# A fused SSM and linear-attention kernel: three quarters of x transposed by DMA on its way in

## Chip, cores and metric

One core of one Trainium2 chip runs the whole computation in one launch. The metric is the device time of the launch in microseconds. The profile's engines are PE (TensorE), PEld (its weight loads), DVE (VectorE), ACT (ScalarE), POOL (GpSimd) and SP (SyncE, which here only issues transfers).

## What is computed

For an input x of 2048 tokens by 512 features in bf16, two branches are mixed by a gate per token.

```python
g = sigmoid((x * gate_w).sum(-1, keepdims=True))
# a: diagonal complex state-space model, 512 states
Bu = einsum("bld,pd->blp", x + 0j, B_bar)
h_t = Lam_bar * h_{t-1} + Bu_t                  # over 2048 tokens
a = 2.0 * einsum("blp,dp->bld", hseq, Cmat).real + x * Dskip
# b: linear attention, 32 heads of 16
q, k, v = split(x @ wqkv)
phi(u) = concat(softmax(u @ w_phi), softmax(-u @ w_phi))
b = (phi(q) @ (phi(k).T @ v)) / (phi(q) @ phi(k).sum(tokens) + 1e-6) @ wo
out = g * a + (1 - g) * b
```

## The kernel before

**Layout.** Tokens are numbered as (a, c, f): a block a of 4, a row c of 128 in it, and a residue f of 4, so token = (a*128 + c)*4 + f. Nearly every product needs x with features on the partitions. That is the tile `xT`, 128 partitions by 4 feature blocks by 2048 token columns; the 512 columns of one residue f stand together, and `tcols(f, a)` names 128 of them. The recurrence over tokens is folded by four: each residue class has its own local products, and a scan runs over the 512 groups.

**Loading x.** Five plain transfers on the SP queue (lines 312, 315, 317) bring x as it stands into `xn`: block 0 in two halves, then blocks 1 to 3, each partition taking four consecutive tokens (4 KB) of a block. Between them stands half of `Wv`, the V part of the projection; its other half is issued on the ACT queue (line 314). `x_block(a)` then transposes each of the 16 tiles of 128 tokens on TensorE, four 128x128 transposes into one PSUM bank (line 431), and a copy by ACT or DVE (lines 373 and 375) puts the bank into `xT`. After the first two tiles of block 0, one matmul on a blank tile `warm` (line 443) is put into PE's list. Six more stand before everything (line 418).

**Other loads.** Behind x, the SP queue holds the DMA transposes of the two B matrices into `BT` (line 321), the small `Wc`, the DMA transposes of the K and Q parts of the projection into `WT` (lines 323 and 324), `Wo` in four parts, and later the DMA transposes of the two C matrices (line 602). Five short parameter vectors go by the ACT queue (line 319), three more by POOL (line 334).

**Work on xT.** `v_unit(ti)` makes V for 128 tokens with four 512-column matmuls (line 457), where f = ti mod 4 and a = ti div 4. The gate needs sixteen one-column matmuls for each residue (line 904). `g_unit(j)` multiplies `BT` by all 512 columns of one residue, for each of the four residues in turn (line 685), and chains them by a diagonal product (line 690). `k_unit` makes the k features (line 797) and their products with V (line 828), `q_unit` the q features (line 888), and `mix` the outputs (lines 997, 1013, 1017, 1029). `fold` prepares the projection weights with w_phi (line 665) from `WT` and a block-diagonal matrix that DVE builds from `Wc`.

**What sets the order.** Every piece is a task with the engines that may run it, its costs, what it waits for, and its buffers. Transfers issued at the start stand for the plan as times, for instance `d_x = [pl.at(t) for t in (3.9, 5.6, 7.0, 8.6, 10.2)]`. The plan does not search: a written list `ORDER` names every task in turn (entry div 2) and its engine (entry mod 2, the first or second of those allowed), and the instructions are put out in that order. Each engine runs its own list in order and waits at the first instruction whose data is missing. The times in the plan choose buffers, but make nothing wait. Buffers named ET are four large tiles: x in natural order holds two of them at first, the tables' scratch and `WT` the other two; the C matrices take one when it is free, and q features use all four later.

Of the kernel before, what the change touches and what calls it, by code (L numbers as in the profile page):

```python
# [18 lines left out]
P = 128  # L19
# [103 lines left out]
def kernel(  # L123
# [48 lines left out]
NDUM = 1  # L172
ORDER = (
    8, 10, 14, 13, 26, 174, 22, 176, 18, 166, 170, 25, 21, 190, 173, 162, 17, 158, 169, 202, 192, 178, 206, 165,
    0, 194, 222, 204, 197, 226, 28, 224, 160, 209, 30, 230, 32, 198, 233, 250, 96, 210, 218, 234, 34, 201, 228,
    36, 40, 38, 214, 252, 180, 42, 242, 134, 212, 236, 44, 238, 46, 216, 4, 186, 136, 2, 48, 90, 59, 240, 254,
    244, 220, 812, 182, 62, 810, 140, 75, 188, 83, 61, 138, 678, 814, 142, 55, 184, 98, 69, 680, 430, 156, 434,
    144, 432, 816, 258, 146, 66, 56, 64, 436, 262, 438, 81, 342, 265, 818, 256, 334, 70, 260, 337, 346, 148, 348,
    338, 554, 150, 341, 444, 446, 344, 152, 52, 440, 154, 6, 450, 443, 356, 358, 360, 350, 382, 352, 354, 87, 388,
    50, 449, 362, 364, 85, 384, 820, 392, 528, 556, 522, 366, 390, 272, 386, 368, 394, 370, 490, 396, 372, 530,  # L180
    456, 398, 524, 458, 374, 532, 274, 400, 452, 496, 526, 376, 534, 78, 536, 460, 404, 822, 470, 538, 276, 406,
    414, 378, 92, 380, 540, 472, 462, 417, 408, 426, 454, 494, 544, 492, 266, 73, 475, 498, 500, 464, 284, 286,
    546, 410, 542, 502, 476, 298, 466, 412, 77, 504, 548, 620, 428, 100, 506, 508, 102, 288, 104, 88, 562, 268,
    468, 624, 614, 652, 512, 514, 622, 278, 618, 300, 106, 270, 516, 518, 616, 478, 290, 110, 626, 108, 280, 520,
    480, 282, 302, 628, 114, 656, 558, 630, 292, 418, 654, 112, 564, 550, 294, 246, 402, 482, 422, 304, 248, 566,
    560, 646, 116, 568, 738, 650, 648, 574, 484, 632, 118, 552, 486, 570, 576, 636, 424, 572, 580, 658, 594, 586,
    740, 296, 122, 742, 582, 660, 420, 638, 744, 584, 578, 306, 120, 746, 710, 94, 126, 686, 488, 596, 588, 598,
    124, 698, 640, 308, 310, 748, 688, 634, 690, 770, 130, 662, 750, 590, 510, 682, 700, 642, 128, 702, 684, 644,
    776, 664, 712, 774, 778, 838, 692, 668, 592, 752, 312, 772, 754, 314, 780, 782, 600, 714, 832, 694, 756, 670,
    704, 844, 672, 834, 760, 696, 602, 330, 842, 846, 784, 318, 706, 840, 132, 604, 666, 762, 850, 332, 836, 716,  # L190
    708, 718, 786, 720, 826, 322, 606, 788, 852, 722, 874, 854, 792, 848, 868, 320, 326, 794, 862, 674, 608, 724,
    764, 324, 796, 828, 872, 830, 328, 676, 766, 726, 768, 798, 800, 864, 878, 856, 876, 610, 866, 860, 728, 804,
    808, 870, 802, 892, 880, 894, 896, 806, 730, 758, 884, 904, 902, 900, 732, 858, 898, 906, 886, 1268, 908, 316,
    1000, 890, 882, 1270, 998, 910, 1036, 914, 996, 916, 1274, 1002, 734, 1272, 888, 918, 912, 1262, 920, 922,
    1028, 1004, 1054, 924, 1006, 930, 1074, 1062, 1030, 1022, 1008, 1010, 1056, 1128, 1130, 1076, 1080, 1024,
    1048, 1132, 1032, 612, 1264, 1050, 1256, 1126, 1058, 1026, 1266, 1078, 1082, 1100, 1102, 1034, 1012, 1052,
    1114, 932, 736, 1040, 1060, 1106, 1014, 1084, 1104, 1088, 1108, 1016, 1110, 1018, 1112, 1134, 1020, 1260,
    1038, 1086, 942, 936, 1116, 1136, 926, 1138, 934, 1066, 1276, 1064, 954, 1278, 1142, 944, 1092, 1118, 1204,
    1206, 1042, 1210, 1230, 1258, 938, 1232, 1068, 1236, 1208, 1212, 1234, 1044, 1214, 1090, 1152, 928, 1144,
    1146, 1158, 966, 1238, 1094, 1178, 1070, 1120, 1216, 940, 1154, 1218, 1122, 1280, 1148, 1096, 1222, 1240,  # L200
    1073, 1184, 1180, 1242, 1156, 946, 1186, 1284, 1166, 1282, 1160, 1244, 968, 1188, 1286, 1192, 948, 1288, 1246,
    1150, 1290, 1162, 1384, 1292, 1098, 1182, 1168, 1248, 1296, 1364, 1164, 1386, 970, 1190, 1358, 1125, 1170,
    1366, 1194, 1298, 1250, 1390, 956, 1300, 1360, 1220, 950, 958, 1392, 1302, 1224, 1368, 1196, 1312, 1046, 1306,
    1388, 1362, 1394, 1314, 1172, 1370, 1308, 952, 1338, 960, 1396, 1226, 1174, 1198, 1252, 1332, 1310, 1376,
    1200, 1372, 962, 1346, 1398, 1316, 1334, 964, 1400, 1318, 1340, 972, 1304, 1402, 1202, 1416, 1374, 1255, 978,
    1418, 1336, 1320, 1342, 1436, 980, 1438, 1344, 1378, 1404, 1324, 974, 1420, 1229, 1410, 976, 1442, 1380, 1348,
    982, 990, 1412, 1322, 1326, 1444, 1440, 1406, 1462, 1350, 1414, 1177, 984, 1383, 992, 1468, 1494, 1422, 986,
    1446, 1450, 1464, 1448, 988, 1470, 1428, 1352, 1328, 1496, 1354, 1488, 1476, 994, 1330, 1472, 1466, 1490,
    1424, 1454, 1474, 1140, 1498, 1409, 1492, 1500, 1480, 1356, 1426, 1478, 1452, 1430, 1433, 1456, 1482, 1435,
    1502, 1485, 1504, 1506, 790, 1294, 1458, 1514, 824, 1508, 1460, 1520, 1487, 1522, 1516, 1510, 1518, 1513, 1524)  # L210
# [18 lines left out]
def _fast_path(ctx, tc, A_x, A_Lambda_re, A_Lambda_im, A_B_re, A_B_im, A_C_re, A_C_im, A_log_dt, A_Dskip,  # L229
# [5 lines left out]
    x4 = A_x[0].rearrange("(a c f) d -> a c f d", f=F, c=P)  # L235
# [64 lines left out]
    xn2 = [wk.tile([P, 2, F, D], BF16, tag=f"ET{k}", name="xn", bufs=1) for k in range(2)]  # L300
    xn = [xn2[a // 2][:, a % 2] for a in range(4)]
# [10 lines left out]
    nc.sync.dma_start(out=xn[0][:, 0:2], in_=x4[0][:, 0:2])  # L312
    for k, q in ((0, nc.scalar), (2, nc.sync)):
        q.dma_start(out=Wv[:, k:k + 2, :], in_=B_wqkv[k * P:(k + 2) * P, 2 * D:3 * D].rearrange("(k p) n -> p k n", p=P))
    nc.sync.dma_start(out=xn[0][:, 2:4], in_=x4[0][:, 2:4])
    for a in range(1, 4):
        nc.sync.dma_start(out=xn[a], in_=x4[a])
# [26 lines left out]
    pl = _Plan({"DVE": 2.4e3, "ACT": 5.0e3, "PE": 1.1e3, "SP": 32.0e3})  # L344
# [10 lines left out]
    early = [pl.held("ET", k) for k in range(4)]  # L355
# [4 lines left out]
    def bfv(b):  # L360
        return b.t[:].bitcast(BF16)[:, 0:512]
# [17 lines left out]
    d_x = [pl.at(t) for t in (3.9, 5.6, 7.0, 8.6, 10.2)]  # L379
    d_wv, d_b, d_wk, d_wq, d_wo, d_ct = (pl.at(t) for t in (5.3, 19.5, 25.5, 30.5, 33.0, 0.0))  # L380
    d_wv0 = pl.at(4.4)
    d_vec, d_wc = pl.at(10.5), pl.at(21.0)
# [38 lines left out]
    xt = {}  # L421
    dums = []

    def x_block(a):
        pl.unit("x_block")
        for f in range(F):
            b = pl.buf(*A1)

            def tr(e, b=b, f=f):
                for kt in range(KT):  # L430
                    nc.tensor.transpose(bfv(b)[:, kt * P:(kt + 1) * P], xn[a][:, f, kt * P:(kt + 1) * P], ident[:])
            t = pl.add({"PE": 460.0} if a == 0 and f < 2 else _pe(4, 128), tr, deps=[d_x[a + (a > 0 or f > 1)]], follow=[t_warm], bufs=[b, early[a // 2]])
            if a == 0 and f < 2:
                dums.append(t)
            xt[a, f] = evac_task(xT[:, :, tcols(f, a)], b, lambda b: bfv(b).rearrange("p (k c) -> p k c", k=KT), [t],
                                 ("ACT", "DVE"), bf=True, rank=9)

        if a == 0:
            bd = pl.buf(*A1)

            def dum(e):
                for _ in range(NDUM):
                    MM(out=bd.t[:], lhsT=warm[:, 0:P], rhs=warm[:], start=True, stop=True)
            t_dum.append(pl.add({"PE": NDUM * 430.0}, dum, follow=dums, bufs=[bd]))

    vt = {}
    t_dum = []

    def v_unit(ti):
        pl.unit("v_unit")  # L450
        f, a = ti % F, ti // F
        b = pl.buf(*A1)

        def mm(k0, k1):
            def fn(e):
                for kt in range(k0, k1):
                    MM(out=f32v(b), lhsT=xT[:, kt, tcols(f, a)], rhs=Wv[:, kt, :], start=(kt == 0), stop=(kt == KT - 1))  # L457
            return fn
        if ti < 2:
            t = pl.add({"PE": 860.0 if ti == 0 else 434.0}, mm(0, 2), deps=[xt[a, f], d_wv0], follow=t_dum, bufs=[b])  # L460
            t = pl.add({"PE": 434.0}, mm(2, 4), deps=[d_wv], follow=[t], bufs=[b])
        else:
            t = pl.add(_pe(4, 512), mm(0, 4), deps=[xt[a, f], d_wv], bufs=[b])
        vt[ti] = evac_task(vx[:, ti, :, 0:Dh], b, lambda b: f32v(b).rearrange("p (h e) -> p h e", e=Dh), [t], ("ACT",), rank=8.5)

    x_block(0)
# [366 lines left out]
    x_block(1)  # L833
    for ti in range(0, 4):
        v_unit(ti)
    x_block(2)
# [858 lines left out]
```

## Time and profile before

| what | value |
|---|---|
| median of 13 runs | 154.75 us (153.97 to 155.31) |
| profiled execution's own time | 155.0 us |
| its span in the profile | 153.0 us |
| PE busy | 145.5 us (95%) |
| DVE busy | 134.3 us (88%) |
| ACT busy | 110.2 us (72%) |
| x transposes on PE, L431 | 64, first at 4.0 us, last at 18.0 us |
| first product with BT, L685 | 21.06 us |

The profile counts from the start of its span. The execution's own time is 2.0 us longer than the span, which lies around it. Busy time of PE overlaps a little with waiting, since the ends of pipelined matmuls are modelled. A busy share alone does not say what a change is worth; for that one has to see which wait ends last in the stage that is changed.

### The profile page before, as it was taken

To read this page: it belongs to the slowest core of one execution; us is meant where nothing else is said; L and a number is where in the kernel's file an instruction comes from. 1 tells how busy PE (TensorE), PEld (TensorE's weight loads), DVE (VectorE), ACT (ScalarE), POOL (GpSimd) and SP (SyncE) were. 2 spreads that over 40 slices of the span, in tenths; PEclk is the share of its full clock that TensorE was granted. 3 is DMA by queue.
4 is the path that set the end of the run, shared out by engine and by line. 5 is a ranking of instruction groups with operands and counts; after the bars stand their busy time and mean duration, and the time that the engine had idled before them with its cause. 6 is when DMAs were issued, how large, how long until landed. Compare 5 with 4: busy or idle time off the path is not lost.

```text
span 153.0 us, 3264 instructions
## 1 busy us (share of the span) xinstructions
PE 145.5 (95%) x1153; PEld 85.8 (56%) x1173; DVE 134.3 (88%) x377; ACT 110.2 (72%) x226; POOL 4.3 (3%) x14
## 2 busy tenths in 40 slices
PE   6989999999999999999999999999999999999990
PEld 1555576745665666655454666656556555555570
DVE  2376998998999999999999899999999999999250
ACT  3048999889897899888889897977774392654030
POOL 8200000000000000000000000000000000000000
PEclk9999999999999999999999999999999999999999
DMA  4999998900003131333703223244132524318631
GB/s 128 358 236 184 156 222 197 181 4 0 0 21 73 47 85 52 109 86 91 98 0 86 73 93 109 81 86 75 34 103 69 73 69 103 94 43 94 150 103 45
DMA packets 31148, 14.95 MB, mean 98 GB/s; under 512 B 23193, under 2 KB 30489, under 8 KB 31129
## 3 DMA queue, kind: packets, MB, share of 16 engines
q1 hardware_dynamic: 29280, 13.20, 40.6%
q10 hardware_dynamic: 1752, 1.51, 3.8%
q8 instruction: 10, 0.16, 0.5%
q14 instruction: 10, 0.07, 0.2%
q0 software_dynamic: 96, 0.00, 0.0%
HBM read 3.17 MB, written 2.10 MB: 34 GB/s over the span
## 4 chain that ended last, share of the span: by engine, by line
PE 82%; DMA 7%; DVE 5%; ACT 1%; issue 1%; SPq 1%; DVEq 0%
PE pp L685 18%; PE pp L1013 17%; PE pp L1029 9%; PE pp L797 9%; PE pp L457 7%; DMA xn<-in_A_x_dram 7%; PE pp L888 5%; PE pp L997 4%; PE pp L690 3%; PE pp L828 3%; PE pp L1017 2%; DVE c L733 2%; PE pp L665 1%; DVE KVbd L870 1%; PE pp L955 1%
## 5 line engine op out<-in xcount | busy, mean ns | idle before, releaser
L685 PE MATMUL pp<-xT,BT 128*128 128x512 bf16 x124 | 31.7, 381 | 0.3
L1000 ACT CAST late<-pp 128x512 bf16<-128x512 f32 x32 | 17.8, 598 | 10.8 <-PE pp L997 10.7
L1013 PE MATMUL pp<-CT,Gs 128*128 128x512 bf16 (+1 forms) x99 | 22.9, 362 | 0.3
L685 PEld LDWEIGHTS <-BT 128*128 128x128 bf16 x128 | 17.8, 145 | 8.8
L242 ACT ACTIVATE E<-pp 128x512 bf16<-128x512 f32 x32 | 17.8, 614 | 2.1 <-PE pp L797 1.5
L242 ACT ACTIVATE ET<-pp 128x512 bf16<-128x512 f32 x32 | 17.7, 604 | 1.0 <-PE pp L888 0.9
L1034 ACT ACTIVATE late<-pp,Gg 128x512 bf16<-128x512 f32 (+1 forms) x15 | 9.5, 669 | 9.8 <-PE pp L1029 9.8
L457 PE MATMUL pp<-Wv,xT 128*128 128x512 bf16 x61 | 15.9, 384 | 0.2
L1029 PE MATMUL pp<-Wo,late 128*128 128x512 bf16 (+1 forms) x67 | 15.7, 366 | 0.1
L888 PE MATMUL pp<-xT,Wq 128*128 128x512 bf16 x62 | 15.5, 379 | 0.1
L797 PE MATMUL pp<-Wk,xT 128*128 128x512 bf16 x63 | 15.2, 379 | 0.1
L373 ACT CAST vx<-pp 128x512 bf16<-128x512 f32 x16 | 9.3, 595 | 7.9 <-PE pp L457 7.9
L1013 PEld LDWEIGHTS <-Gs 128*128 128x128 bf16 x104 | 9.4, 98 | 7.3 <-DVE Gs L773 0.5
L373 ACT CAST Gs<-pp 128x512 bf16<-128x512 f32 x21 | 12.2, 603 | 1.7 <-PE pp L690 1.7
L1004 DVE TENSOR_TENSOR late<-late 128x512 bf16<-128x512 bf16 x32 | 12.4, 422 | 0.0
L997 PE MATMUL pp<-KVbd,ET 128*128 128x128 bf16 x128 | 10.7, 219 | 0.0
L997 PEld LDWEIGHTS <-ET 128*128 128x128 bf16 x128 | 8.6, 98 | 3.4 <-issue 0.2
L797 PEld LDWEIGHTS <-xT 128*128 128x128 bf16 x64 | 6.1, 98 | 6.7
L821 DVE TENSOR_TENSOR E<-E,rc 128x2048 bf16<-128x2048 bf16 x8 | 9.7, 1220 | 0.1
L888 PEld LDWEIGHTS <-Wq 128*128 128x128 bf16 x64 | 5.9, 97 | 6.3
L733 DVE TENSOR_TENSOR_SCAN c<-sp,c 128x512 bf16<-128x512 f32 x8 | 9.3, 1210 | 0.0
L457 PEld LDWEIGHTS <-xT 128*128 128x128 bf16 x64 | 5.9, 99 | 5.7 <-DVE xT L375 0.2
(173 smaller groups left out, 254.5 us busy)
## 6 DMA issues: line engine op xcount, KB each, us to landing
Zs<-c SPq DMA_DIRECT2D x32, 64.0 KB, 2.1
xn<-in_A_x_dram SPq DMA_DIRECT2D x3, 512.0 KB, 5.2
out_dram<-late ACTq DMA_DIRECT2D x9, 128.0 KB, 2.0
c<-c SPq DMA_DIRECT2D x16, 64.0 KB, 2.0
CT<-ET SPq DMA_DIRECT2D x8, 128.0 KB, 3.6
out_dram<-late SPq DMA_DIRECT2D x6, 128.0 KB, 2.0
xn<-in_A_x_dram SPq DMA_DIRECT2D x2, 256.0 KB, 4.4
Wo<-in_B_wo_dram SPq DMA_DIRECT2D x4, 128.0 KB, 2.6
```

What stands on the lines that cost most here:

```text
L242: return nc.scalar.activation(**kw)
L373: nc.scalar.copy(out=o, in_=view(b))
L457: MM(out=f32v(b), lhsT=xT[:, kt, tcols(f, a)], rhs=Wv[:, kt, :], start=(kt == 0), stop=(kt == KT - 1))
L685: MM(out=f32v(b), lhsT=BT[:, kt].rearrange("p r (q t) -> p (r q) t", t=NT)[:, :, j + 4 * h], rhs=xT[:, kt, f * NCH:(f + 1) * NCH], start=( ...
L733: nc.vector.tensor_tensor_scan(out=bw_.t[:, ri], data0=rb, data1=b1.t[:, ri], initial=0.0, op0=ALU.mult, op1=ALU.add)
L797: MM(out=f32v(b), lhsT=xT[:, kt, tcols(f, a)], rhs=Wk2[:, kt, :], start=(kt == 0), stop=(kt == KT - 1))
L888: MM(out=f32v(b), lhsT=Wq2[:, kt, g * P:(g + 1) * P], rhs=xT[:, kt, f * NCH:(f + 1) * NCH], start=(kt == 0), stop=(kt == KT - 1))
L997: MM(out=f32v(pn[sgn])[:, g * P:(g + 1) * P], lhsT=ets[f].t[:, sgn, g, cs], rhs=KVbd[:, sgn, g, :], start=True, stop=True)
L1000: tn = pl.add(_act(512), lambda e, sgn=sgn: nc.scalar.copy(out=o2.t[:, sgn], in_=f32v(pn[sgn])), deps=[t], bufs=[pn[sgn], o2], rank=rank + 2)
L1004: VT(out=v, in0=v, in1=als[f].t[:, a, sgn * H:(sgn + 1) * H].rearrange("p (g h) -> p g h", g=HG).unsqueeze(2).to_broadcast([P, HG, Dh, 8]) ...
L1013: MM(out=f32v(py)[:, 0:w], lhsT=st, rhs=CT[:, tt // 2 + 4 * (tt % 2), n * w:n * w + w], start=(tt == 0), stop=False)
L1029: MM(out=f32v(py)[:, 0:w], lhsT=oT.t[:, g, :], rhs=Wo[:, g, hs], start=False, stop=(g == HG - 1))
```

## The change

Only one residue class of x is loaded as it stands: f = 0, in two halves on the SP queue, 1 KB for each token, its four blocks transposed on TensorE as before. The other three residue classes come as DMA transposes straight from HBM into their 512 columns of `xT`, one transfer each on the SP queue. Both halves of `Wv` go on the ACT queue, ahead of the vectors there. The blank matmul in the middle is dropped. `xn` needs one ET tile instead of two, so one is free from the start. The plan's times are changed, and the list `ORDER` is a new one for all tasks.

```diff
-    xn2 = [wk.tile([P, 2, F, D], BF16, tag=f"ET{k}", name="xn", bufs=1) for k in range(2)]
-    xn = [xn2[a // 2][:, a % 2] for a in range(4)]
+    xn = wk.tile([P, F, D], BF16, tag="ET0", name="xn", bufs=1)
...
-    nc.sync.dma_start(out=xn[0][:, 0:2], in_=x4[0][:, 0:2])
-    for k, q in ((0, nc.scalar), (2, nc.sync)):
-        q.dma_start(out=Wv[:, k:k + 2, :], in_=B_wqkv[k * P:(k + 2) * P, 2 * D:3 * D].rearrange("(k p) n -> p k n", p=P))
-    nc.sync.dma_start(out=xn[0][:, 2:4], in_=x4[0][:, 2:4])
-    for a in range(1, 4):
-        nc.sync.dma_start(out=xn[a], in_=x4[a])
+    x0 = xf[0].rearrange("(a c) d -> c a d", c=P)
+    for h in range(2):
+        nc.sync.dma_start(out=xn[:, 2 * h:2 * h + 2], in_=x0[:, 2 * h:2 * h + 2])
+    for k in (0, 2):
+        nc.scalar.dma_start(out=Wv[:, k:k + 2, :], in_=B_wqkv[k * P:(k + 2) * P, 2 * D:3 * D].rearrange("(k p) n -> p k n", p=P))
+    for f in range(1, F):
+        nc.sync.dma_start_transpose(out=xT[:, :, f * NCH:(f + 1) * NCH], in_=xf[f])
...
-    d_x = [pl.at(t) for t in (3.9, 5.6, 7.0, 8.6, 10.2)]
-    d_wv, d_b, d_wk, d_wq, d_wo, d_ct = (pl.at(t) for t in (5.3, 19.5, 25.5, 30.5, 33.0, 0.0))
+    d_x = [pl.at(t) for t in (4.1, 4.9, 7.7, 10.2, 12.7)]
+    d_wv0, d_wv, d_b, d_wk, d_wq, d_wo = (pl.at(t) for t in (4.9, 5.7, 18.0, 21.0, 23.3, 26.0))
...
+    xt = {(a, f): d_x[1 + f] for f in range(1, F) for a in range(4)}
...
+    for a in range(4):
+        b = pl.buf(*A1)
+
+        def tr(e, b=b, a=a):
+            for kt in range(KT):
+                nc.tensor.transpose(bfv(b)[:, kt * P:(kt + 1) * P], xn[:, a, kt * P:(kt + 1) * P], ident[:])
...
+        xt[a, 0] = evac_task(xT[:, :, tcols(0, a)], b, lambda b: bfv(b).rearrange("p (k c) -> p k c", k=KT), [t],
+                             ("ACT", "DVE"), bf=True, rank=9)
```

Here `xf[f]` is the residue class f of x in HBM: 512 rows of 1 KB, 4 KB apart. In the new file the lines move: the transposes are L426, the V products L443, the products with BT L670.

## The prediction

> **What bounds the kernel now.** I read the page's parts 1 and 2 first, to see which engine is full and when.
>
> ```profile
> PE 145.5 (95%) x1153; PEld 85.8 (56%) x1173; DVE 134.3 (88%) x377; ACT 110.2 (72%) x226; POOL 4.3 (3%) x14
> PE   6989999999999999999999999999999999999990
> DVE  2376998998999999999999899999999999999250
> ```
>
> PE is full from the fourth slice on, DVE almost as full from the fifth. Only the head, about the first 12 us, shows slack, and there it is in both. Then the chain that ended last, at its start:
>
> ```profile
> 1.66 4.39 DMA xn<-in_A_x_dram
> 6.06 5.64 DMA xn<-in_A_x_dram
> 11.75 0.40 PE pp L431 x4
> ...
> 12.52 0.55 PE pp L431 x8
> 13.07 2.59 PE pp L457 x12
> ...
> 20.82 0.38 PE pp L904 x16
> 21.20 0.93 PE pp L685 x4
> ```
>
> The chain is the load of x until 11.75 us, and from there PE without a break: transposes (L431), the V products (L457), gate columns (L904), and at 21.20 the first product with BT (L685). Eight transposes take 0.55 us, so 0.069 us each; twelve V matmuls take 2.59, 0.216 each. Third, busy time by stage (columns: stretch, its length, busy time of PE, PEld, DVE, ACT, POOL, granted clock, DMA share, GB/s):
>
> ```profile
> 4.00:8.00 4.00, 3.75 (x31) 2.33 (x31) 1.27 (x3) 0.00 (x0) 0.95 (x2) 1.00 1.03 357
> 8.00:12.00 4.00, 3.23 (x32) 1.93 (x30) 2.78 (x12) 2.37 (x5) 0.00 (x0) 1.00 1.09 230
> 9.50:11.30 1.80, 1.66 (x15) 0.98 (x16) 1.32 (x9) 1.08 (x3) 0.00 (x0) 1.00 1.20 160
> 12.75:17.25 4.50, 4.50 (x30) 2.26 (x28) 4.12 (x20) 4.15 (x11) 0.00 (x0) 1.00 1.20 128
> 20.25:22.00 1.75, 1.75 (x29) 1.17 (x27) 1.68 (x9) 1.75 (x3) 0.00 (x0) 1.00 1.28 288
> 60.00:80.00 20.00, 19.89 (x106) 11.19 (x107) 19.54 (x37) 17.53 (x39) 0.00 (x0) 1.00 0.37 80
> ```
>
> The 4 to 8 row is plain loads (357 GB/s), the 20.25 row a DMA transpose alone (WT, 288 GB/s); in 12.75 to 17.25 transposes of BT run with a dip (128), and in 9.5 to 11.3 transposes run beside the end of the x loads (160). The clock is 1.00 throughout, so it changes nothing.
>
> ```profile
> PEld L431 <- DMA xn<-in_A_x_dram: 3.4, 5, 1.0
> ...
> L375 DVE COPY xT<-pp 128x512 bf16<-128x512 bf16 x11 | 4.3, 421 | 3.1 <-PE pp L431 3.1
> L373 ACT COPY xT<-pp 128x512 bf16<-128x512 bf16 x5 | 2.9, 584 | 0.2 <-PE pp L431 0.2
> ```
>
> The first row is who waited for x; the other two are the copies of transposed x out of PSUM, 421 ns on DVE and 584 on ACT.
>
> **What the change takes off PE.** 48 of 64 transposes: 48 x 0.069 = 3.3 us. One warm matmul (L443), about 0.3 us. And the order of arrival: now PE waits for x tile by tile. Between 4 and 12 us it did 44 transposes (3.0), 12 V matmuls (2.6) and the warm one (0.2): 5.8 us of work at full rate in 8.0 us.
>
> I place the new list step by step, from its own order (entries halved are task numbers, so the residue of each V product can be counted). The first half of x residue 0 is as many bytes as the first load was, so the start is about 4.1. Sixteen transposes: 1.03 us for the first eight in the timeline, 0.62 for the next eight, to 5.75. Fourteen V matmuls of residue 0 (3.0, and 0.45 for the first two, which took 0.89 before) to 9.2. Parameter products, 0.4, to 9.6. Then residue 1: six matmuls, 1.3, to 10.9. Residue 2: eight, 1.7, to 12.6. A gate (0.38) and four of residue 1 to 13.9. Residue 3 is first needed here; four matmuls, two gates, eight, a gate and four more give 18.5, where the first BT product stands. By then 48 V matmuls and 4 gates are done. Before, the chain had 44 and 2 at 21.20; with four more matmuls (0.86) and two gates (0.76) the same work would end at 22.8. Head start: 4.3 us.
>
> **What it adds: will the data be there?** x residue 0 and Wv are 1.05 MB plain. The row of the first 12 us says 357 GB/s after 4.0, and 0.56 MB had come by 4.0, so they end near 5.4. A residue is 0.52 MB. [...] Rows first: WT alone at 288 GB/s is 1.8 us a residue; at the 183 GB/s of the C loads (24.6 to 30.75 us, dips included) it is 2.9. [...] The trace shows 288 at best. I take 2.2 us, nearer to the clean row, because the sources differ only in row pitch. WT has a pitch of 3 KB, these have 4 KB; no row shows 4 KB.
>
> With 2.2 us and 0.5 for landing (an estimate), residues 1, 2, 3 are there at 8.1, 10.3, 12.5 and needed at 9.6, 10.9, 13.9. BT follows in two clean 1.8 and a dip of 2.5 (the 12.75 row moved 0.58 MB in 4.5 us, 2.0 at 288 GB/s; what causes it the trace does not tell): 6.1, so 18.6 against 18.5. WT's first half, 20.8 to 22, is needed near 23. So the waits are 0 to 1.5 us in all (1.8 to 2.7 us a residue). If the rate is better, nothing is gained: PE has no idle time left to give.
>
> **Queues that are moved.** SP issues transposes in 1.70 to 5.10 us each, and three more stand ahead of BT, Wc, WT, Wo and C. SP next serves an engine's result after 30 us, and has waits of 15.4 us there, so that is covered; but Wc comes with BT, and DVE's block-diagonal step waits for it in order. On ACT's queue the second half of Wv stands before the five vector loads: 0.44 us later each, last issue near 5.4, and ACT must then copy two x blocks (0.58 each) that PE wants at 7.0. If the queue is full, ACT comes at 6.5 and PE waits about 0.7. The parameter product needs the vectors at 9.2; before it ran at 12.07, so 2 us of cover stay. POOL's three loads are untouched. C now goes to a free buffer instead of one that held x; SP waited 1.4 us there and nobody waited for SP, so 0.
>
> **DVE and ACT.** DVE loses nine copies of 0.421, 3.8 us; the other reassignments (Gs one more, Wq and c one less each at 0.69, three scalings of 0.25 more) cancel to 0.1. Its parameter chain starts at about 9.6 instead of 12.57. So DVE, full from there, can follow by 3 to 3.7 us, less than PE's 4.3. ACT loses three copies and has 28% free.
>
> **Sum.** 4.3 less 0.8 (DVE following, 0.6; waits for ACT, residue 2 and BT, half of 0.7 falling beside the former) = 3.5 us. The end is alike: last matmuls to last output and barrier took 4.3 us. The profiled execution took 155.0 us, 2.0 over its span of 153.0; 155.0 - 3.5 = 151.5, and the median of the runs lies 0.25 below that execution: 151.2.
>
> **Rivals.**
> 1. *Part of the head start is spent in the middle.* V products are PE's filler when it waits for the k features. Before, 20 V matmuls stood after 54 us (4.3 us of filler); now 12 do (2.6). If DVE sets the pace there, PE idles up to 1.7 us. For it: DVE 19.54 of 20 in the 60 to 80 row. Against: DVE's list is shorter too. 151.2 + 1.7 = 152.9.
> 2. *Slower: the x transposes crawl.* Reading rows at 4 KB pitch, or beside Wv on ACT's queue, they may run at the 160 GB/s of the mixed row: 3.3 us a residue. Then BT is there at 5.9 + 9.9 + 6.1 = 21.9, PE waits 3.4 us and the gain is just gone: that is the deciding point. At 4.0 us a residue the wait is 5.5 and the time 153.2 + 3.5 = 156.7 (151.2 + 5.5). Against: Wv ends near 5.4, so the mix lasts about 1 us, and 3 KB pitch ran at 288.
> 3. *Not what it says.* The three loads could have fallen apart into element copies; the built list shows three transposes of 128x4x512 on SP, so no chance is kept for this.
>
> **Numbers.** A change under 0.2% (0.3 us) can't be told from none here. Likeliest case, 150.2 to 152.4 around 151.2: 0.62. Rival 1 and a partial form of 2 (2.7 to 3.1 us a residue), 152.4 to 154.4: 0.19. Gain and waits cancel: 0.03. Rival 2 in full, 0.12, and some wait of the new order that I have not found, 0.04: slower, 0.16. Faster 0.81. Range 150.0 to 155.2: it leaves out 0.04 below and about 0.13 above.
>
> **What would show it.** Right: L426 with 16 transposes from 4.1, first L670 at 18 to 19.5, PE with no idle time over 0.5 us between 6 and 140, vp on DVE near 9.6, three transposes at 250 to 290 GB/s between 5 and 12. Wrong: PE waits named "DMA xT" at the first matmuls of residue 2 or 3, or "DMA BT" before L670, summing to over 3.5 us (rival 2); or PE idle between 55 and 95 behind DVE (rival 1).

## The result, and the profile after

The changed kernel took 154.09 us in the median of 11 runs (153.01 to 154.44), the kernel before 154.94 beside it; the ratio is 0.9941, interval 0.9924 to 0.9958. So it is 0.6% faster, 0.9 us, where 3.5 were predicted. Run again beside other experiments on another chip it gave 154.19 and a ratio of 0.9954 (0.9932 to 0.9975). The profiled execution of the changed kernel took 154.59 us, its span is 152.5. One run of e5, below, 156.65 us, fell in a slower state of the chip and is left out of its ratio.

From parts 1 and 2 of the page of the changed kernel (busy time, share of the span and instructions; then PE's tenths in 40 slices):

```profile
PE 141.9 (93%) x1104; PEld 82.8 (54%) x1124; DVE 129.2 (85%) x370; ACT 110.1 (72%) x221; POOL 4.3 (3%) x14
PE   6889969999999999999999999999999999999950
```

PE lost 3.6 us of busy time, as the change should make it (each of the two traces lacks 20 matmul records), and DVE 5.1, where 3.8 were expected. But look at the two ends. PE's third to sixth digits are 8, 9, 9, 6 (the sixth slice is 19 to 23 us), and its last two are 5 and 0, where the kernel before has 9 and 0. The chain that ended last is empty on this page, so the ends are read from busy time by stretch (columns as before: stretch, length, PE, PEld, DVE, ACT, POOL, granted clock, DMA share, GB/s):

```profile
4.00:8.00 4.00, 3.27 (x26) 1.95 (x26) 1.36 (x8) 1.07 (x2) 0.94 (x2) 1.00 1.16 301
8.00:12.00 4.00, 3.20 (x22) 1.52 (x22) 1.27 (x11) 1.52 (x4) 0.00 (x0) 1.00 0.73 141
10.00:11.00 1.00, 0.87 (x11) 0.61 (x12) 0.31 (x4) 0.00 (x0) 0.00 (x0) 1.00 0.01 2
15.50:19.30 3.80, 3.75 (x60) 2.37 (x60) 3.77 (x17) 3.80 (x8) 0.00 (x0) 1.00 1.24 139
60.00:80.00 20.00, 19.89 (x118) 11.00 (x119) 19.08 (x36) 18.69 (x42) 0.00 (x0) 1.00 0.35 77
```

From 10 to 11 us the DMA engines moved 2 GB/s: a microsecond without a transfer, in the middle of the loads that PE is waiting for. From 15.5 to 19.3 they moved 139 on average, in the transpose of the second B matrix. Between 4 and 12 us PE is busy for 6.47, where the kernel before has 6.98: the head has not become fuller. In the middle of the kernel (60 to 80) PE is as full as before, 19.89 of 20.

What PE waited for from 3 to 25 us (engine, line, and for what; total, times, longest), first in the profile of the changed kernel, then the first row of the same view in the profile of its second run (e9):

```profile
PE pp L670 <- ACT vx L371: 1.2, 1, 1.2
PE pp L478 <- DMA vec_n<-in_A_Dskip_dram: 0.7, 1, 0.7
PE pp L426 <- DMA xn<-in_A_x_dram: 0.7, 2, 0.5
```

```profile
PE pp L670 <- DMA BT<-in_A_B_im_dram: 1.1, 1, 1.1
```

Three waits in the head: for the second half of x's plain residue (L426), for the parameter rows (L478), and before the first product with BT (L670). The first profile puts the last one down to ACT, whose copy happened to end at 20.86. But the semaphore of BT_im, the second of the two B matrices, was complete at 20.79, and L670 starts at 20.92, 0.13 us later; in the second run, whose profile names BT_im, it is 0.14 (20.48 and 20.62). The forecast was 18.5. The kernel before has no wait of PE for the rows or for BT. From 23 us to the last matmul the same view lists no wait of PE at all.

The SP queue's timeline (start, duration, issues) and its wait, both of the changed kernel:

```profile
1.76 10.02 SPq L315 DMA_TRANSPOSE xT<-in_A_x_dram  x3
11.82 1.72 SPq L319 DMA_TRANSPOSE BT<-in_A_B_re_dram  x1
13.59 2.70 SPq L319 DMA_TRANSPOSE BT<-in_A_B_im_dram  x1
```

```profile
SPq L315 <- DMA xT<-in_A_x_dram: 1.7, 1, 1.7
```

SP stood still for 1.7 us at the third x transpose, until the first one was reported complete, at 9.7 us, though its data had been through at 7.5. In the traces of before and of the changed kernel the transfers of SP and ACT mark their completion on eight semaphores in all, 101 and 103 to 109, over and over. With seven loads on ACT (two of Wv, five parameter rows, on 104, 106, 107, 108, 101, 103 and 104) the third transpose has the same one as the first, 105, and waits for it: the first one's last mark on 105 comes at 9.69, the third is issued at 9.71. That is the empty microsecond. The last three rows on ACT's queue wait for semaphores in the same way. Two of them are issued at 4.17 and 5.68 us, 0.02 after the halves of x's plain residue have put their last marks on 101 and 103 (PE's transposes of the halves start at 4.20 and 5.71); the last, whose 104 has its last mark at 4.68, follows them at 5.97.

The second B matrix met something else. The first row below is a stretch within its transpose, the second is from the DMA queues between 15 and 19.5 us (packets, MB, share of 16 engines):

```profile
17.50:18.70 1.20, 1.20 (x22) 0.73 (x20) 1.20 (x7) 1.20 (x3) 0.00 (x0) 1.00 0.12 6
q8 instruction: 1, 0.02, 1.7%
```

For 1.2 us the DMA engines moved 6 GB/s, although the transpose had been issued by 16.29. The packet of the instruction queue q8, 16 KB, ran from 16.80 to 18.04. The prediction's "dip" in the kernel before is the same: 4 GB/s from 15.0 to 16.2 us, after such a packet that ran from 14.62 to 15.67. In these two profiles and in those of e3, e8 and e9 the packet starts well inside the transpose of BT_im, and its data take 3.6 to 4.3 us; in e1, where they were through before the packet came, they took 2.4. No run moved the packet, so that it stops the transpose is read from the times alone.

Last the end, from the timeline of the changed kernel, and the DMA queues between 148.1 and 149.7 us (packets, MB, share of 16 engines):

```profile
145.90 0.22 PE L1046 MATMUL pp<-ident,fb 128*1 128x128 bf16 x1
146.05 1.05 PE L1011 MATMUL pp<-Wo,late 128*128 128x256 bf16 x8
146.16 0.28 DVE L1049 TENSOR_REDUCE ff<-pp 1x1 f32<-1x128 bf16 x1 [5.41 <-PE pp L1046]
146.76 0.88 DVE L1018 TENSOR_SCALAR late<-pp,Gg 128x256 bf16<-128x256 f32 x2
147.27 0.34 ACTq L1022 DMA_DIRECT2D out_dram<-late  x1
```

```profile
q10 hardware_dynamic: 144, 0.07, 14.7%
q1 hardware_dynamic: 135, 0.06, 13.6%
q14 instruction: 3, 0.02, 5.8%
q8 instruction: 1, 0.02, 5.3%
```

The validity flag (its transpose L1046, its reduction L1049) is now done ahead of the last output's evacuation (L1018). In the kernel before it was the last thing PE and DVE did. And the two instruction queues, q8 with one packet of 16 KB and q14 with three of 8 KB, run here among the packets of the last output (q1 and q10). From the start of the last output matmul to the end of the span it is 5.7 us (146.82 to 152.5); before it was 4.5 (148.47 to 153.0).

### The profile page after: what moved, and what is told of

Read it like the earlier page. It is cut to its first block, busy times and chain, and to the rows that moved or that the text cites. A ratio compares the mean times of both kernels' runs of the same rounds, so it can differ in the third digit from the quotient of the medians.

```text
span 152.5 us, 3159 instructions
## 1 busy us (share of the span) xinstructions
PE 141.9 (93%) x1104; PEld 82.8 (54%) x1124; DVE 129.2 (85%) x370; ACT 110.1 (72%) x221; POOL 4.3 (3%) x14
## 4 chain that ended last, share of the span: by engine, by line
## 5 line engine op out<-in xcount | busy, mean ns | idle before, releaser
L670 PE MATMUL pp<-xT,BT 128*128 128x512 bf16 x123 | 31.6, 380 | 1.5 <-ACT vx L371 1.2
L995 PE MATMUL pp<-CT,Gs 128*128 128x512 bf16 (+1 forms) x101 | 23.4, 362 | 0.2
L670 PEld LDWEIGHTS <-BT 128*128 128x128 bf16 x128 | 17.8, 145 | 10.4 <-issue 1.7
L1016 ACT ACTIVATE late<-pp,Gg 128x512 bf16<-128x512 f32 x15 | 10.2, 689 | 13.6 <-PE pp L1011 10.9
L443 PE MATMUL pp<-Wv,xT 128*128 128x512 bf16 x61 | 15.2, 379 | 0.2
L371 ACT CAST Gs<-pp 128x512 bf16<-128x512 f32 x20 | 11.6, 584 | 2.8 <-PE pp L675 1.7
L979 PE MATMUL pp<-KVbd,ET 128*128 128x128 bf16 x128 | 10.7, 219 | 0.1
L371 ACT CAST vx<-pp 128x512 bf16<-128x512 f32 x16 | 8.8, 596 | 2.2 <-PE pp L443 2.2
L443 PEld LDWEIGHTS <-xT 128*128 128x128 bf16 x64 | 5.8, 97 | 6.5 <-DVE xT L373 0.4
```

What stands on the lines that cost most here:

```text
L371: nc.scalar.copy(out=o, in_=view(b))
L670: MM(out=f32v(b), lhsT=BT[:, kt].rearrange("p r (q t) -> p (r q) t", t=NT)[:, :, j + 4 * h], rhs=xT[:, kt, f * NCH:(f + 1) * NCH], start=( ...
L979: MM(out=f32v(pn[sgn])[:, g * P:(g + 1) * P], lhsT=ets[f].t[:, sgn, g, cs], rhs=KVbd[:, sgn, g, :], start=True, stop=True)
L995: MM(out=f32v(py)[:, 0:w], lhsT=st, rhs=CT[:, tt // 2 + 4 * (tt % 2), n * w:n * w + w], start=(tt == 0), stop=False)
L1016: nc.scalar.mul(out=ot.t[:, hs], in_=f32v(py)[:, 0:w], mul=Gg[:, ti:ti + 1])
```

## The experiments

All are edits of the changed kernel. Where the order is edited, the list that chooses buffers and engines stays, and a copy `EMIT` sets in which order the instructions are put out (an entry halved is a task). The table is read as a whole at the end; "full clock" is when the trace's record of granted clock at 1.00 begins, "tail" is from the start of the last output matmul to the end of the span, both of the one profiled execution. In the changed kernel the record at 1.00 lasts from 4.95 to 151.72 us, and 0.50 follows it. Ahead of 4.95 the trace has no record, but there the six blank matmuls of 512 columns start about 427 ns apart, where V's at 6.9 to 9.0 us start 216 apart, and the first eight transposes about 107, where the next eight start 56 apart. This slower rate is called half clock here. The ratios compare with runs of the kernel before that were made beside each.

| kernel | median us (runs) | ratio to before, interval | first L670 | full clock from | tail |
|---|---|---|---|---|---|
| before | 154.94 (48) | 1 | 21.06 | 5.84 | 4.5 |
| changed | 154.09 (11) | 0.9941 (0.9924 to 0.9958) | 20.92 | 4.95 | 5.7 |
| changed, again (e9) | 154.19 (12) | 0.9954 (0.9932 to 0.9975) | 20.62 | 5.29 | 5.6 |
| e1 rows on POOL | 153.62 (12) | 0.9925 (0.989 to 0.996) | 20.27 | 9.17 | 6.1 |
| e2 params later | 153.38 (6) | 0.9906 (0.9875 to 0.9937) | 20.02 | 7.03 | 5.7 |
| e3 last store on SP | 154.29 (12) | 0.9956 (0.9933 to 0.9979) | 20.51 | 4.01 | 5.7 |
| e4 V before BT | 154.03 (12) | 0.9953 (0.9933 to 0.9974) | 21.65 | 10.00 | 5.6 |
| e5 blank matmuls | 154.45 (12) | 0.9983 (0.9968 to 0.9998) | 20.37 | 4.46 | 5.7 |
| e6 old end | 152.77 (5) | 0.9866 (0.9845 to 0.9887) | 20.68 | 4.40 | 4.5 |
| e7 rows, blank | 153.13 (6) | 0.9907 (0.9871 to 0.9942) | 19.40 | 5.39 | 6.1 |
| e8 rows, blank, old end | 151.75 (5) | 0.9802 (0.9779 to 0.9825) | 20.16 | 5.94 | 4.8 |
| e10 rows, old end | 152.22 (6) | 0.9849 (0.98 to 0.9899) | 18.99 | 4.99 | 4.8 |
| e11 = e8 again | 151.4 (6) | 0.9779 (0.9748 to 0.9809) | 19.04 | 6.58 | 4.8 |
| e12 e8 and V first | 151.45 (6) | 0.9799 (0.9757 to 0.9841) | 19.82 | 3.94 | 4.8 |

### e1: the parameter rows on GpSimd's queue

```diff
-    for n, src in enumerate(vsrc):
-        nc.scalar.dma_start(out=vec_n[4 * n:4 * n + 4, :], in_=src.rearrange("(j p) -> j p", p=P))
...
     make_identity(nc, ident[:])
+    for n, src in enumerate(vsrc):
+        nc.gpsimd.dma_start(out=vec_n[4 * n:4 * n + 4, :], in_=src.rearrange("(j p) -> j p", p=P))
+    for n in range(3):
+        nc.gpsimd.dma_start(out=vq[:, n, :], in_=vsrc[n].rearrange("(q t) -> q t", t=2 * NT))
...
-    for n in range(3):
-        nc.gpsimd.dma_start(out=vq[:, n, :], in_=vsrc[n].rearrange("(q t) -> q t", t=2 * NT))
```

> The five parameter-vector loads leave the ACT queue for POOL's, right behind the identity matrix. Theory T (the head is set by when BT lands; the third x transpose waits 1.7 us on SP for the first one's completion mark, because the eight marks are handed out in turn and the five vector loads use them up): the third x transpose is issued near 8.0 instead of 9.7, BT lands 1.0 us earlier, the first L670 starts near 19.8 instead of 20.9, and the time falls from 154.1 to about 153.1. Rival R1 (each stop of PE in the head counts by itself): the vector wait of 0.7 us goes too, 153.4 or lower by that alone. Rival R2 (a later engine sets the end, so a head start is lost again): 154.1 whatever L670 does.

The SP queue of e1, whose wait for the first transpose is gone:

```profile
1.76 8.50 SPq L315 DMA_TRANSPOSE xT<-in_A_x_dram  x3
10.30 2.04 SPq L317 DMA_TRANSPOSE BT<-in_A_B_re_dram  x1
12.38 2.46 SPq L317 DMA_TRANSPOSE BT<-in_A_B_im_dram  x1
```

BT is issued 1.2 to 1.5 us earlier, the gap between the second and third transpose is gone from the DMA packets, and PE's only wait in the head is 0.6 us for x's second half. So the wait on a shared semaphore was the cause of the gap. But the median fell by 0.5 only, where 1.0 was expected, and the twelve runs are two groups: six from 152.75 to 153.2, six from 154.04 to 154.79. The profiled execution, 154.04, is of the upper one. What is slow in it is PE itself; its V products between 6.4 and 9 us (busy, mean ns of one):

```profile
L443 PE MATMUL pp<-Wv,xT 128*128 128x512 bf16 x6 | 2.8, 634 | 0.0
```

634 ns is what the 512-column matmuls ahead of the record of full clock take in the changed kernel too (379 inside it), and only six were done in 2.6 us where the changed kernel's profile has thirteen. The fourteen V matmuls took 4.50 us, not 3.22, and the eight transposes before them 1.04, not 0.62. The record of granted clock agrees: full only from 9.17 us. The clock column of the view by stretch does not show it. It reads 1.00 (third number from the end) here too, where four matmuls fill a microsecond:

```profile
7.00:8.00 1.00, 1.00 (x4) 0.40 (x3) 1.00 (x6) 0.34 (x1) 0.80 (x1) 1.00 0.99 203
```

### e2: six V matmuls ahead of the parameter products

```diff
+EMIT = list(ORDER)
+EMIT.remove(162)
+EMIT.insert(EMIT.index(26), 162)
+EMIT.remove(158)
+EMIT.insert(EMIT.index(26), 158)
...
-        self.order = [self.tasks[v >> 1] for v in ORDER]
+        self.order = [self.tasks[v >> 1] for v in EMIT]
```

> PE does six more V matmuls before the parameter products, so that these no longer stop it while the vectors are under way; buffers stay as they were. T: PE comes 0.7 us earlier to the first L670 and waits there 1.9 us instead of 1.2, L670 starts at 20.9 as before, time unchanged (154.1, within 0.2). R1: 0.7 us faster, 153.4. R2: unchanged as well, but with L670 at 20.2.

It took 0.7 us off the median: 153.38, what R1 gave (153.4), and not T's 154.1. In its profile the wait for the rows is gone, and none for BT is left: BT_im was complete at 19.88, earlier than in the changed kernel, and L670 followed at 20.02. So the wait for the rows was worth filling, but one profile doesn't tell how much of the gain is that and how much is BT's earlier arrival, which the edit does not touch.

### e3: the last store ahead of the flag on SP

```diff
-    1462, 1459, 1432, 1434, 1465, 1461, 1466)
+    1462, 1459, 1432, 1434, 1465, 1460, 1467)
```

> The last two output halves change queues: the first goes by SP, the last by ACT, so that no transfer stands behind the flag load on SP. T (1.1 us of the lead is lost behind the last matmul, because the last 64 KB are issued behind the flag load): 0.5 to 0.9 us faster, 153.2 to 153.6, with the end 4.3 to 4.8 us after the last L1011 instead of 5.4. If the tail's length comes from something else (a slow landing): within 0.2 of 154.1.

No gain. This edit lets SP store the first half of the last output before it loads the flag, and ACT the second. The order did change: the packets of SP's store were through by 148.04. But then it was ACT's that was late. Eight of its 128 packets ran at 149.5 to 149.96, after the 16 KB packet of 1.44 us that had started at 148.11 on the instruction queue. SP's last wait is the same line in the changed kernel and here; in the kernel before it is 0.5 us in all:

```profile
SPq L162 <- SPq L162: 2.0, 2, 1.5
```

The theory that SP's order costs the microsecond fell.

### e4: one V tile ahead of the first product with BT

```diff
+EMIT = list(ORDER)
+EMIT.remove(178)
+EMIT.insert(EMIT.index(378), 178)
+EMIT.remove(204)
+EMIT.insert(EMIT.index(178), 204)
```

> One V product of four matmuls (0.86 us), which stood behind the first three products with BT, is put before them, and the ACT copy that frees its bank is put before a table step. T: PE works 0.86 of the 1.2 us that it waits for BT; L670 starts at 20.9 as before and all behind it comes 0.86 earlier: 153.2. If the bank is what PE waits for there and not BT: no gain, 154.1 or slower. R2: 154.1.

No gain over the changed kernel (0.9953 against 0.9941 and 0.9954). Entry 178 is the V tile, four matmuls; 204 is the copy that frees its bank. The wait for BT is gone from its profile, but that execution started its full clock at 10.0 us (its V products between 6.4 and 9 us take 635 ns), so PE was late by itself and the comparison says little about the wait.

### e5: blank matmuls while x is awaited

The kernel before had one blank matmul among the first transposes and the change drops it. In the profiles so far PE stands for 0.55 to 1.1 us between the eighth and the ninth transpose, and the clock's start lay anywhere from 4.0 to 10.0 us. All records of full clock last 139.9, 143.4 or 146.8 us, which differ by 3.41. The author's theory, which no run shows as such: the clock goes full behind a stretch of 3.41 us with little idle time of PE, so a stretch that contains the gap may not do, and then half clock lasts another 3.41 us.

```diff
         def tr(e, b=b, a=a):
+            for _ in range(3 * (a == 2)):
+                MM(out=f32v(b)[:, 0:256], lhsT=warm[:, 0:P], rhs=warm[:, 0:256], start=True, stop=True)
             for kt in range(KT):
```

> Edit: three matmuls of 256 columns on zeros, put between the eighth and the ninth x transpose, where TensorE waited 0.65 to 0.9 us for x's second half in every profile of the changed kernel and of the first four experiments. Clock theory: the granted clock goes full at the end of the first stretch of 3.41 us (the full-clock records last 139.9, 143.4 or 146.8 us, which differ by 3.41) in which TensorE idled less than about 0.9 to 1.0 us; the moment varies with each run's phase, 4.0 to 7.0 us after the start where no stretch is lost, 9.0 to 10.4 where one is (9.17 and 10.0 us in two of the profiles so far, 4.0 to 7.0 in the others and in the kernel before, which kept a blank matmul there). With the blank matmuls the profile's full clock begins at 7.1 us at the latest in every run. Since TensorE then only arrives earlier at the waits for the vector rows (0.74) and for BT (1.2), the median moves by 0 to 0.4: 153.7 to 154.1. Rival (the clock costs the head the whole of its lost work): about 0.4 of the runs lose 2 us, so the median falls by 0.8 or more, under 153.3.

A miss for both: 154.45, if anything slower. The blank matmuls bring nothing while PE waits for the rows and for BT afterwards; whether the 0.3 us on top are real is open.

### e6: the end of the order list as it was before

```diff
-        self.order = [self.tasks[v >> 1] for v in ORDER]
+        self.order = [self.tasks[v >> 1] for v in EMIT]
...
     1279, 1357, 772, 1448, 1305, 1468, 1406, 1450, 1452, 1378, 1454, 1430, 1380, 1408, 1382, 1470, 1472, 1456,
-    1462, 1459, 1432, 1434, 1465, 1461, 1466)
+    1462, 1458, 1432, 1434, 1464, 1460, 1467)
+EMIT = list(ORDER)
+EMIT[-10:] = [1456, 1462, 1432, 1434, 1470, 1458, 1460, 1464, 1472, 1467]
```

> Edit: the end of the order list as the kernel before had it: the flag's transpose after the last output matmul on TensorE, the flag's reduction after it on VectorE, both last 256-column halves evacuated on ScalarE, the first stored by SP and the second by ScalarE. Tail theory: in the changed kernel the flag was done at 146.6, a microsecond ahead of the last evacuation, so the engines reached the branch on the flag early and the instruction queues' packets (one of 16 KB and three of 8 KB) ran at 148.5 to 149.7, among the last output's; 5 to 8 packets of it on one DMA engine landed 1.4 us late (150.3 for the others' 148.9 to 149.3). In the kernel before the same packets ran at 151.2, with all outputs landed by 150.5. So last matmul to end goes from 5.4 back to about 4.3: median lower by 0.8 to 1.2, 152.9 to 153.3, and the instruction packets run after the last output's packets. Rival (the tail is longer for another reason, such as the evacuation on VectorE or the landing of the stores as such): the flag's path merely comes later, no gain, 154.1 or above.

152.77, 1.3 us less, a little more than the 0.8 to 1.2 that were expected. The end of e6 in the timeline, and its DMA queues from 147.7 to 148.5 us, then from 148.9 to 150.2:

```profile
145.76 1.42 ACT L1018 ACTIVATE late<-pp,Gg 128x512 bf16<-128x512 f32 x3 [0.18 <-PE pp L1013]
146.52 0.22 PE L1048 MATMUL pp<-ident,fb 128*1 128x128 bf16 x1
146.78 0.28 DVE L1051 TENSOR_REDUCE ff<-pp 1x1 f32<-1x128 bf16 x1 [6.30 <-PE pp L1048]
147.20 0.34 ACTq L1024 DMA_DIRECT2D out_dram<-late  x1
```

```profile
q1 hardware_dynamic: 162, 0.07, 33.8%
q10 hardware_dynamic: 144, 0.07, 28.7%
```

```profile
q14 instruction: 3, 0.02, 5.8%
q8 instruction: 1, 0.02, 4.7%
```

Both halves of the last output are through by 148.42, and only then come the instruction packets, as in the kernel before. The tail is 4.5 us again. The edit moves flag, evacuations and stores together, so it shows that the new end costs 1.2 us; that the instruction packets do it is read from where they lie. In the changed kernel and in e1 to e5, e7 and e9 they start before the last store is through, and that store's packets stretch over 1.4 to 1.9 us (tails 5.6 to 6.1); in before, e6, e8 and e10 to e12 they start after it, and it takes 0.4 (tails 4.5 to 4.8).

### e7 and e8: the rows on GpSimd with blank matmuls, without and with the old end

The edits are those of e1 and e5 (e7), and of e1, e5 and e6 (e8).

> Edit: the five vector rows on GpSimd's queue (as in e1_vec_on_pool) and the blank matmuls of e5_blank. e1's twelve runs fell into two groups, six at 152.75 to 153.2 and six at 154.04 to 154.79; its profile was of the slow group and had the full clock only from 9.17 us. Clock theory: with no wait for the rows or for BT left, the start of the full clock is what sets the head; the blank matmuls take the late start away, so all runs lie at 152.6 to 153.3, median 152.8, and the profile shows the full clock by 7.1 us and the first BT product at 18.5 to 19.2 instead of 20.27. Rival (the two groups come from the DMA side, e.g. from when the transposes land): two groups as before, a spread of 2 us, median about 153.6.

> Edit: e7_pool_blank and the end of the order list of e6_tail. If the losses are the rows with the third transpose's wait behind them, the late clock, and the flag's place at the end, they add up: e7's median less 1.0 for the tail, 151.6 to 152.0, about the 151.2 that was predicted for the change. Rival (one of them merely moves the wait on, such as the middle's VectorE or filler work taking up the lead): not under e7's by more than 0.3, about 152.6 or above.

e7: five of six runs lie at 152.91 to 153.24, one at 154.65, and the median, 153.13, is 0.3 above the expected one; the full clock starts at 5.39, L670 at 19.40. e8: 151.75, the sum that was expected. In e8's profile PE still waits for BT_im, 1.0 us.

### e9 to e12: the changed kernel again, e8 without blank matmuls, e8 again, and a V tile first

e9 is the changed kernel, e10 has the edits of e1 and e6, e11 is e8, e12 is e8 with the edit of e4. That is one V tile of four matmuls (52 V matmuls stand ahead of the first BT product, 48 in e11), not the two that its expectation names.

> The changed kernel unaltered, beside the other runs of this call, since e5_blank (154.45, ratio 0.9983 to the kernel before) came out 0.4 us slower than the changed kernel on another chip (154.09, 0.9941). If that was the chip, this reads 154.3 to 154.6 here; if the blank matmuls cost 0.4 us, 154.1.

> Edit: e8_pool_blank_tail without the blank matmuls (the vector rows on GpSimd's queue, the end of the order list as in the kernel before). Clock theory: about four runs in ten start the full clock at 9.0 us or later and lose up to 1.5 us, so the runs fall into two groups, about 151.5 to 152.2 and 152.7 to 153.4, and the median is 0.3 to 0.9 above e11's. Rival (the blank matmuls change nothing; e1's two groups had another cause): the same spread and median as e11_pool_blank_tail_again, within 0.2.

> The same kernel as e8_pool_blank_tail, run again beside e10 and e12 for more executions: 151.4 to 152.4 as before, median 151.75, one group.

> Edit: e8_pool_blank_tail, with the two further V tiles (eight matmuls of 512 columns, 1.7 us) put ahead of the first BT product on TensorE as in e4_v_before_bt. e8's profile still shows TensorE waiting 1.0 us there for BT_im, which landed at 20.1. Theory (what is left in the head is BT's arrival): the V tiles fill the wait, median 0.5 to 0.9 under e11's, 150.9 to 151.3. Rival (the products L672 come later by the V tiles' 1.7 us and VectorE, which waits for them, then sets the pace): no gain or up to 0.7 slower, 151.8 to 152.5.

e10 against e11 is the test of the clock. e10's six runs are two groups again: 151.19, 151.53, 151.63 and 152.81, 153.27, 153.36. e11's six are one: 151.14 to 151.69. Six runs each are few, and the intervals of the two ratios touch. Over all kernels with the rows on GpSimd, nine of eighteen runs without blank matmuls (e1, e10) lie in an upper group some 1.5 us above the lower, and two of twenty-three with them (e7, e8, e11, e12). The V products between 6.4 and 9 us in the profiled execution of e10 (151.19); in that of e11 (151.31) they take 381 ns:

```profile
L445 PE MATMUL pp<-Wv,xT 128*128 128x512 bf16 x14 | 3.2, 380 | 0.0
```

Both are at full clock, as executions of the lower group should be. No upper-group execution of e10 was profiled; e1's is the only one. The others can be placed by an estimate. All full-clock records last 139.9, 143.4 or 146.8 us (146.77 in before and in the changed kernel), that is 41, 42 or 43 times 3.413, and the mean granted clock of a profiled run is below 1 by half the share of its span that lies behind that record (in the changed kernel 151.72 to 152.48, which gives 0.9975; its mean reads 0.998). So each run's span and mean clock give where its record ended, and with that its start up to a multiple of 3.4 us; for the eleven profiled runs of the changed kernel and its variants whose mean is below 1 this comes within 0.2 us of the trace. The nine runs of the lower groups of e1 and e10 come out at 4.0 to 5.5 us, the nine of the upper groups at 5.9 to 7.3, or at 9.3 to 10.8, where e1's profiled one is. The groups do not overlap, as the theory of a clock that starts late in some runs would have it. With blank matmuls, e11's profiled run starts at 6.58 and is still in the lower group, 151.31. Two runs with blank matmuls, 154.65 of e7 and 152.89 of e12, stay unexplained.

e12 brought nothing (151.45, where 150.9 to 151.3 was expected if BT's wait were left): in e11's own profile PE waits 0.2 us in the head and not for BT, so there was no wait left to fill. e8's 1.0 us was of that execution: its BT_im transpose stood beside a 16 KB instruction packet at 16.5 us, e11's was nearly through when that came at 17.0. e9 says that the changed kernel is 154.1 to 154.2 here too, which speaks against the chip as the reason for e5's 0.3 us; but the intervals of the two ratios overlap. e8 and e11, one kernel, are 2.0% and 2.2% under before (1.8 to 2.5 by the two intervals); no edit that was tried is faster beyond the noise.

## Why the prediction was wrong, and where it was right

The size was wrong, 0.9 us for 3.5, and it was wrong in two steps. The step that orders the arrivals in the head, with "2 us of cover stay" for the parameter rows and BT at 18.6 us, gave PE a net lead of 3.5 us; the changed kernel has about 2. The step "the end is alike" put the end at nothing; it costs 1.2. Two less 1.2 is about the 0.9 that was measured. The lead is an estimate from the weight loads on PE (1124 in the changed kernel, 1173 before, 20 more than matmul records in both; taken as one for each matmul): at full rate, the matmul work left in the changed kernel is 1.6 to 2.1 us less than in the kernel before, at 24 us as at 60, 100 and 140.

That the range held the result is luck: it fell where the range allowed for slow transposes and for idle time in the middle, and neither came. The transposes themselves did what was forecast. With the rows on GpSimd, blank matmuls and the old end (e11), the lead at 24 us is 3.8 and the median 151.4, near the predicted 151.2, with x loaded just as the change does. No run gave these edits to the kernel before; its profile has no wait for rows or BT that they could take away, and its end is already the old one.

- **Start and rate: right.** L426 began at 4.20 (4.1 predicted). The three transposes moved their data in 5.4 to 7.5, 7.5 to 10.1 and 11.0 to 13.3 us, 2.1 to 2.6 us each where 2.2 was taken, and PE never waited for one. That is 0.13 to 0.16 us for each 128x128 tile. In their best microseconds (6 to 7 and 12 to 13) 286 and 291 GB/s were moved, about the 288 of WT in the kernel before, whose plain loads had 357. Rival 2, crawling transposes, fell.
- **DVE, ACT and the middle: right.** PE has no wait from 23 us to its last matmul, and the lead at 24 us is about that at 140. Rival 1, the head start spent in the middle, fell. Of the 0.8 that the sum takes off (its parts, 0.6 and half of 0.7, make 0.95), the part for ACT's copies was not needed: PE has no wait for them, and the full queue that it was put in for is not shown by any run.
- **"2 us of cover stay" for the parameter rows: wrong.** They were wanted at 9.4 and PE waited 0.7. The step counted 0.44 us of delay on ACT's queue; ACT's last three rows stood behind waits for semaphores as well and were issued at 4.2, 5.7 and 6.0, and the one that PE waited for landed at 10.1. vp, the first step of DVE's parameter chain, came at 10.7, not 9.6.
- **The arrival of BT: wrong by 2.2 us.** The data of x's third transpose were through at 13.3, 1.3 later than the forecast implies, 1.0 of it the empty microsecond, and BT was complete 1.4 us after its data, where 0.5, an estimate of the author's, was taken. The step said that SP's longer issue list was covered because nobody waits for SP early; it looked for who waits for SP and not for what SP waits for. BT's data took 6.1 us as predicted, but only because the dip of the kernel before came again: beside the instruction packet the second matrix took 3.9. In e1, which has neither gap nor dip, both took 4.5 and BT was complete at 16.97. How much of PE's 1.2 us wait is the semaphore and how much the packet is not separated.
- **x's second half: 0.4 late.** Transposes ended at 6.2, not 5.75, as PE waited 0.5 for it.
- **The dropped blank matmul: costed at a gain of 0.3, wrong sign once the rest is mended.** In the changed kernel it is hidden behind the other waits (e5). With these gone its absence costs about 1.5 us in half the runs (e10 against e11, 0.8 in the median). The line in the prediction that the clock is 1.00 throughout and changes nothing was read from a column that does not show the start: the kernel before has full clock only from 5.84 us.
- **"The end is alike": wrong by 1.2 us.** The largest single term. The new order list moved the flag ahead of the last evacuation; e6 takes 1.3 us off by undoing that and what goes with it.

Together: 1.3 for the end (e6 against the changed kernel), and 1.0 to 1.4 for rows, semaphore and clock (e6 against e8 and e11), which the runs do not split further. That is 2.3 to 2.7 of the 2.9 us missing between 154.1 and 151.2.

## What to carry to other kernels

When a load is moved or split, list for every queue what its next issue has to wait for, shared completion semaphores included (one of them held SP for 1.7 us here), and not only who waits for its data. A gap in TensorE's first few microseconds can cost more than its length: here 0.65 us of gap went with about 1.5 us in half the runs, by the estimate those with a late start of full clock. Fill it, and judge that by the spread of many runs, as one profile shows one start only. A new order list must be read to its last entry: here a flag that was done early went with instruction packets among those of the last store, 1.2 us.

## What the hardware showed that was not expected

- The start of full clock lay between 3.9 and 10.0 us in fourteen profiled executions whose first matmul came at about 1.3 us. Counted from the start of one matmul to that of the next (0.43 us for 512 columns at half clock), PE was idle for at most 0.90 us in the 3.41 us ahead of it (the step between the lengths of the full-clock records), and for at least 1.05 in the 3.41 us ahead of those, in all fourteen (time ahead of the span is taken as idle). The closest readings are e2, where full clock followed 0.90 us of idle time (3.6 to 7.0 us), and e1, where it did not follow 1.05 (2.3 to 5.8); that is no measured threshold. The busy columns, with their modelled ends, do not order the stretches so: full clock did not follow 0.64 of idle time in e1, and did follow 0.74 in e12.
- A packet of an instruction queue behind the first microsecond of these profiles is 8 or 16 KB and takes 0.3 to 1.9 us (0.31 to 1.59 in before and in the changed kernel, 1.44 for that of e3 at 148.11). Where it runs beside the last store, 8 of the store's 128 packets end 0.8 to 1.5 us after the others (in the changed kernel at 150.34, the others by 149.26). In the head, a stop of about 1.2 us in a DMA transpose goes with it (6 GB/s from 17.5 to 18.7 us in the changed kernel, 4 from 15.0 to 16.2 before).
- A DMA transpose was reported complete 0.5 to 2.9 us after its data had moved: 2.2 for the first of x in the changed kernel (7.5 and 9.7 us), 1.4 for BT_im there, 0.5 for it in e1, 2.9 in e6.
